# A ring of five half supergroups for x, one buffer for transposed channels, and all second weights in the ring

## The chip, the cores and the metric

The kernel runs on one core of one Trainium2 chip. Its five engines have their own instruction queues: PE (matrix multiply, with PEld for its weight loads), DVE (vector), ACT (scalar), POOL and SP, which here issues all transfers. The metric is the time of one execution on the device in microseconds (us).

## The reference

Two layers follow one another, in float32. The first is a causal convolution whose seven taps are different for every token and head; the second is a soft mixture of experts over all 28672 tokens.

```python
# x [8, 3584, 192], weight_gen [8, 3584, 8 heads, 7 taps]
w = softmax(weight_gen, axis=-1)
out[b, s, h, :] = sum_k w[b, s, h, k] * x_pad[b, s + k, h, :]      # 24 channels a head

x = out.reshape(28672, 192)
logits = x @ phi                                                    # 32 slots, 4 for each of 8 experts
slot_input = softmax(logits, axis=0).T @ x                          # over the tokens
slot_out[e] = relu(slot_input[e] @ w1[e]) @ w2[e]                   # 192 -> 1024 -> 192
return softmax(logits, axis=1) @ slot_out
```

## The kernel before

**Units of work.** A block is 26 tokens. A *group* is four blocks, 104 tokens, and a batch has 35 groups, so there are 280. Seven groups make a *supergroup* (40 of them, `s`), the piece in which x and the taps are loaded. Two neighbouring groups make a *pair* `p`, on which the engines work. Eight pairs make a *unit* `u` for the experts' softmax over tokens; the last two units have six.

**x.** The convolution is a matmul: `conv(p)` (L227 to 240) multiplies a band matrix of taps by 32 rows of x for each block. Heads are handled four at a time on 128 partitions, so x stands block-diagonally: head h of four on partitions 32h to 32h+31, in its own fourth of the columns, and zeros elsewhere. The zeros are written once (L138 to 141 and L394 to 397), and `loadx` (L170 to 174) overwrites the diagonal with four transfers of 32 rows. The tile `big` has room for two supergroups of x. A supergroup is loaded in two parts: part 0 is groups 0 to 3 (100 KB a transfer), part 1 groups 4 to 6 (75 KB). A part of supergroup s+2 goes where that part of s was, once PE has read it.

**Taps.** `loadw(s)` brings the taps of a supergroup into one of four buffers. From there a chain runs over several engines: `tap_top` (DVE, L184: maximum over seven taps), `tap_spread` (POOL, L190), `tap_rows` (PE, L196), `tap_sub` (DVE, L201), `tap_exp` (ACT, L205), `band_make` (POOL, L214), which writes one of three band buffers in halves.

**From a convolution to the experts.** `conv(p)` writes one of three PSUM buffers `cv`, p modulo 3. ACT takes the softmax denominators from it (L248), DVE inverts them (`conv_inv`, L254), and `conv_out(p)` (DVE, L259) divides and stores the pair as `tm`, after which `cv` is free for `conv(p + 3)`. PE transposes the pair (`xpose`, L273), ACT copies the result into `cm` (L278), the transposed channels of a unit, of which there are two buffers. When a unit is complete, `logits` (PE, L302) reads `cm`, the maximum is updated, and `dispatch` (L366) accumulates the slots' inputs.

**What sets the order.** The first pairs are written out by hand (from L377). The stream after that is a list of operations with a cost, what they read and what they write. A planner runs through it four times with these costs and then issues every operation at its planned time. PE's and SP's order is that of the list; DVE's, ACT's and POOL's is the planner's. On the chip each engine goes through its queue in order and waits on semaphores, so an instruction that waits holds up all that stand behind it. SP's transfers share eight landing semaphores in turn, so a transfer also waits for the landing of the one issued eight places before it. In the list, step k handles pairs 2k and 2k+1, and the loads for which x or taps buffers come free at that step stand in it:

```python
if part == 1 and s + 5 < NSG:
    op(SP, 0.4, [], [("w", (s + 5) % NTAP), ("r", (s + 5) % NTAP)], loadw, s + 5, late=4.2)
if s + 2 < NSG:
    op(SP, 1.8, [], [x_of(s, part)], loadx, s + 2, part, late=2.2)
```

**The end.** The second weights w2 of seven experts are loaded into `big` as x leaves it (`loadw2`, L454), those of the eighth into a tile of their own, `w2l` (L704 and 705). After the experts (L781), `big` serves a third time, as a ring of output buffers: PE makes output columns, DVE and ACT copy them into `big` (L809), SP sends them out.

## Time and profile before

| | |
|---|---|
| median of 3 runs | 349.42 us (348.41 to 350.35) |
| profiled execution: its own time, its span | 349.6 us, 347.9 us |
| mean granted clock of TensorE | 0.942 |
| PE, DVE, POOL, ACT busy | 311.6, 251.3, 215.3, 159.5 us |
| x loads: 160 of 100 KB, 160 of 75 KB | 3.5 and 4.1 us to landing (median) |
| taps loads: 40 of 392 KB | 4.4 us to landing (median) |

The span has a first fill (to some 30 us), the stream of pairs (to 260 us), the experts (to 286 us), and the output (to the end). In rows of groups, the columns are line, engine, operation, tiles and shapes, count, busy time and mean; an idle time in square brackets in a timeline row is that of the engine before the row, with what ended it. A row of a timeline may merge several instructions (x2). A matmul in float32 leaves two records, so `conv(p)`, sixteen matmuls, shows as x32, and a group as x16.

### The profile page before, as it was taken

How to read it: one execution, taken by the hardware profiler on the slowest of the kernel's cores; microseconds unless marked ns; L12 is line 12 of the kernel's file. 1: busy time of each engine (PE TensorE's matmuls, PEld its weight loads, DVE VectorE, ACT ScalarE, POOL GpSimd, SP SyncE). 2: the span in 40 equal slices, each digit the busy share in tenths (PEclk: the TensorE clock that was granted, in tenths of full speed). 3: DMA queues.
4: the chain of work that ended last, by engine and by line, in shares of the span. 5: the costliest groups of instructions: out<-in, count | busy, mean ns of one | idle time of the engine just before them, and what ended most of it. 6: DMA issues, size and time to landing. Idle time of an engine off the chain costs nothing.

```text
span 347.9 us, 16181 instructions
## 1 busy us (share of the span) xinstructions
PE 311.6 (90%) x6800; PEld 218.0 (63%) x6800; DVE 251.3 (72%) x550; ACT 159.5 (46%) x425; POOL 215.3 (62%) x259
## 2 busy tenths in 40 slices
PE   8799899989999999998999989899998789999810
PEld 6477777768777777786786867677776453233200
DVE  7677678787888888788887778777765639766520
ACT  6354355555556445645555435454550316344310
POOL 8699659879699878879797687796503610000000
PEclk9899999999999999999999999999999989886855
DMA  6887777858777867878768768665379009999995
GB/s 196 239 222 233 217 216 213 229 146 234 226 213 235 234 181 192 206 231 225 201 179 222 226 186 242 187 196 149 105 286 412 32 2 367 400 402 398 400 401 209
DMA packets 32856, 80.80 MB, mean 232 GB/s; under 512 B 7056, under 2 KB 7184, under 8 KB 32784
## 3 DMA queue, kind: packets, MB, share of 16 engines
q1 hardware_dynamic: 32784, 79.77, 72.9%
q8 instruction: 54, 0.88, 1.1%
q14 instruction: 18, 0.15, 0.1%
HBM read 57.38 MB, written 22.36 MB: 229 GB/s over the span
## 4 chain that ended last, share of the span: by engine, by line
PE 58%; DMA 13%; DVE 9%; POOL 6%; ACT 4%; issue 3%; SPq 3%; DVEq 0%; ACTq 0%; POOLq 0%
PE cv L238 22%; PE pt L273 11%; PE ls L302 6%; DMA out<-big 6%; PE pmx L196 6%; PE acb L366 5%; POOL band L214 4%; DMA taps<-wh 4%; PE po L802 4%; DMA big<-xh 4%; SPq L811 2%; PE so L781 2%; DVE tm L259 1%; DVE big L809 1%; SPq L174 1%
## 5 line engine op out<-in xcount | busy, mean ns | idle before, releaser
L214 POOL TENSOR_TENSOR band<-taps,mask 128x588 f32<-128x588 f32 (+3 forms) x158 | 139.2, 912 | 27.3 <-ACT taps L205 24.8
L238 PE MATMUL cv<-big,band 128*26 128x100 f32 x4480 | 117.4, 250 | 8.8 <-DMA big<-xh 4.7
L238 PEld LDWEIGHTS cv<-big,band 128*26 128x26 f32 x4480 | 95.7, 104 | 39.3 <-issue 30.5
L259 DVE TENSOR_TENSOR tm<-cv,ws 128x384 f32<-128x384 f32 x140 | 73.0, 551 | 6.5 <-DVE ws L254 0.5
L278 ACT COPY cm<-pt 128x312 f32<-128x312 f32 x140 | 52.1, 423 | 41.9 <-PE pt L273 41.1
L248 ACT ACTIVATE ws<-cv,eps 128x16 f32<-128x16 f32 x140 | 38.1, 273 | 64.0 <-PE cv L238 51.7
L273 PE MATMUL pt<-ident,tm 122*128 122x122 f32 x420 | 60.0, 279 | 0.7 <-ACT cm L278 0.7
L273 PEld LDWEIGHTS pt<-ident,tm 122*128 122x128 f32 x420 | 44.0, 142 | 17.7 <-issue 14.7
L802 PE MATMUL po<-cT,so 32*128 32x442 f32 (+3 forms) x256 | 44.4, 701 | 3.1 <-DVE big L809 2.0
L254 DVE RECIPROCAL ws<-ws 128x32 f32<-128x32 f32 x70 | 24.1, 344 | 27.1 <-ACT ws L248 26.5
L809 DVE COPY big<-po 128x936 f32<-128x936 f32 (+1 forms) x24 | 26.2, 1096 | 16.8 <-DMA out<-big 7.5
L809 ACT COPY big<-po 128x936 f32<-128x936 f32 (+1 forms) x24 | 21.8, 918 | 33.4 <-DMA out<-big 15.1
L190 POOL TENSOR_TENSOR spread<-own,top 128x392 f32<-128x392 f32 x37 | 31.3, 847 | 6.9 <-PE pt L273 2.8
L196 PE MATMUL pmx<-spread,near 128*128 128x392 f32 x80 | 34.3, 510 | 0.9 <-DVE maskT L391 0.7
L802 PEld LDWEIGHTS po<-cT,so 32*128 32x128 f32 (+1 forms) x256 | 14.2, 182 | 32.2 <-DVE big L809 14.8
L184 DVE TENSOR_REDUCE top<-taps 128x56 f32<-128x392 f32 x40 | 22.2, 556 | 11.2 <-DMA taps<-wh 9.2
L302 PE MATMUL ls<-cm,phi_sb 128*32 128x208 f32 (+1 forms) x576 | 28.6, 333 | 0.0
L366 PE MATMUL acb<-tm,dt 128*32 128x193 f32 x536 | 26.0, 328 | 1.0 <-issue 0.7
L205 ACT ACTIVATE taps<-taps 128x392 f32<-128x392 f32 x40 | 21.0, 525 | 9.9 <-DVE taps L201 9.8
L201 DVE TENSOR_TENSOR taps<-taps,pmx 128x392 f32<-128x392 f32 x40 | 22.1, 553 | 1.5 <-PE pmx L196 1.1
L79 POOL TENSOR_TENSOR LT<-LT,rm 128x576 f32<-128x576 f32 (+1 forms) x16 | 18.1, 1136 | 7.1 <-DVE rm L77 5.2
L91 POOL TENSOR_TENSOR LT<-LT,sm 128x576 f32<-128x576 f32 (+1 forms) x16 | 18.2, 1136 | 6.5 <-DVE sm L89 4.5
(113 smaller groups left out, 253.3 us busy)
## 6 DMA issues: line engine op xcount, KB each, us to landing
big<-xh SPq DMA_DIRECT2D x160, 100.0 KB, 3.5
taps<-wh SPq DMA_DIRECT2D x40, 392.0 KB, 4.4
big<-xh SPq DMA_DIRECT2D x160, 75.0 KB, 4.1
out<-big SPq DMA_DIRECT2D x24, 468.0 KB, 6.5
out<-big SPq DMA_DIRECT2D x24, 442.0 KB, 6.6
big<-w SPq DMA_DIRECT2D x7, 768.0 KB, 8.5
w1a_sb<-w1a SPq DMA_DIRECT2D x16, 256.0 KB, 4.6
w1b_sb<-w1b SPq DMA_DIRECT2D x8, 256.0 KB, 3.9
```

The costliest lines, as they stand in the source:

```text
L190: eng.tensor_tensor(out=tops[s][0], in0=own.to_broadcast([128, KT, NBC]), in1=tops[s][1].rearrange("p l o -> p o l").to_broadcast([128, KT ...
L196: P.matmul(pmx[:, 0:TAPS], near, tops[s][0].rearrange("p q l -> p (q l)"), start=True, stop=True)
L214: eng.tensor_tensor(out=w[:, :, z].rearrange("p b (a k) -> p b a k", k=k), in0=r[:, :, :, 0:k].to_broadcast([128, hi - lo, a, k]), in1=m[: ...
L238: P.matmul(cv[32 * blk : 32 * blk + T, o : o + 4 * GX], bands[s % NBAND][:, bc // 2, :, bc % 2], xb[:, :, bc * GX : (bc + 1) * GX], start= ...
L248: A.activation(wss[p // 2][:, p % 2], cvs[p % NCV][:, 0 : 16 * GX].rearrange("p (h w) -> p h w", w=GX)[:, :, GW:], AF.Identity, bias=eps[: ...
L259: V.tensor_tensor(out=tms[u % NTM][:, pr, 1 : 2 * D + 1].rearrange("p (h w) -> p h w", w=GW), in0=cv[:, :, 0:GW], in1=wss[p // 2][:, p % 2 ...
L273: P.transpose(pt[:, i, 0:TR], tm[0:TR, pr, 1 + 128 * i : 129 + 128 * i], ident[0:TR, 0:TR])
L278: copy(cms[u][:, pr].rearrange("p i b j -> p (i b) j"), pts.pop(p).rearrange("p i (b j) -> p (i b) j", j=32)[:, :, 0:T])
L302: P.matmul(lp[32 * blk : 32 * blk + 32, 0:n, par, 0:T], phi_sb[:, 2 * par + i, :], cm[:, 0:n, 1 if i else 2 * par, blk, :], start=(i == 0) ...
L366: P.matmul(ac[32 * q : 32 * q + 32], dt[:, g, :], tm[:, g // 2, o : o + D + 1], start=(g < 4), stop=(g + 4 >= 2 * n))
L802: P.matmul(po[dst : dst + hi - lo, q % 2, 0 : n * T], so[32 * q : 32 * q + 32, lo:hi], cT[32 * q : 32 * q + 32, g0 : g0 + n, 0:T], start=T ...
L809: (V.tensor_copy if done[1] % 2 else A.copy)(ot.rearrange("p (q c) -> p q c", q=2), po[:, :, 0 : n * T])
```

## The change

The tile `big` now holds five halves of a supergroup, numbered j = 2s + part, each 28 of the 56 block-columns (3.5 groups, 87.5 KB a transfer). `loadx(j)` fills slot j modulo 5. The first five halves are loaded before the stream, and half j + 5 goes where half j was. The fourth group of a supergroup now reads from two halves. The zeros of the fifth slot are four more operations, two on POOL and two on ACT. `big` grows by a quarter, from 44800 to 56000 bytes a partition. `cm` has one buffer instead of two, which frees 9984 bytes. All eight second weights go into `big` (12288 of its 14000 columns), and `w2l` is gone. The output ring has 14 buffers where it had 11.

```diff
-    XB = 4 * NBC * GX
-    big = keep.tile([128, 2 * XB], F32, name="big")
+    NXH, HBC = 5, NBC // 2
+    XB = 4 * HBC * GX
+    big = keep.tile([128, NXH * XB], F32, name="big")
...
-    xbd = [big[:, i * XB : (i + 1) * XB].rearrange("p (h c) -> p h c", h=4) for i in range(NXB)]
+    xbd = big.rearrange("p (i h c) -> p i h c", i=NXH, h=4)
...
-    def loadx(s, part):
-        xb = xbd[s % NXB]
-        z = slice(0, 8 * SGH * GX) if part == 0 else slice(8 * SGH * GX, NBC * GX)
+    def loadx(j):
+
+        s, part = divmod(j, 2)
+        z = slice(part * HBC * GX, (part + 1) * HBC * GX)
         for h in range(4):
-            SY.dma_start(xb[32 * h : 32 * h + 32, h, z], xh[s, h, :, z])
+            SY.dma_start(xbd[32 * h : 32 * h + 32, j % NXH, h], xh[s, h, :, z])
...
-                             xb[:, :, bc * GX : (bc + 1) * GX], start=True, stop=True)
+                             xbd[:, j % NXH, :, b * GX : (b + 1) * GX], start=True, stop=True)
...
-            cms[u] = pa.tile([128, UP, 3, 4, T], F32, tag="cm", name=f"cm{u}")
+            cms[u] = pa.tile([128, UP, 3, 4, T], F32, tag="cm", name=f"cm{u}", bufs=1)
...
+    for h in (0, 1):
+        G.memset(xbd[:, 4, h], 0.0)
...
+    for h in (2, 3):
+        A.copy(xbd[:, 4, h], zero.to_broadcast([128, HBC * GX]))
     band_make(0, 16, HB, V)
+    loadx(4)
     loadw(4)
...
         for s in range(NSG):
             for part in range(2):
-                if max(1, (SGG * s + (SGH, SGG)[part] - 1) // 4) != k:
+                j = 2 * s + part
+                if max(1, (SGG * s + (3, 6)[part]) // 4) != k:
                     continue
...
-                if s + 2 < NSG:
-                    op(SP, 1.8, [], [x_of(s, part)], loadx, s + 2, part, late=2.2)
-                elif s == NSG - 2 and part == 1:
-                    op(SP, 2.0, [], [x_of(s, 0), x_of(s, 1)], loadw2, 0, XB // WE, late=8.0)
+                if j + NXH < 2 * NSG:
+                    op(SP, 1.8, [], [x_of(j)], loadx, j + NXH, late=2.2)
+                elif j + 2 < 2 * NSG:
+                    i = j + NXH - 2 * NSG
+                    op(SP, 1.0, [], [x_of(j)], loadw2, i * XB // WE, (i + 1) * XB // WE)
...
-    op(SP, 2.0, [], [x_of(0, 0), x_of(0, 1), x_of(1, 0), x_of(1, 1)], loadw2, XB // WE, E - 1)
+    op(SP, 2.0, [], [x_of(j) for j in range(NXH)], loadw2, 3 * XB // WE, E)
...
-    w2l = pc.tile([128, WE], F32, name="w2l", bufs=1)
-    SY.dma_start(w2l, w2[:, E - 1])
...
-    OT = 2 * XB // (2 * 18 * T)
+    OT = NXH * XB // (2 * 18 * T)
```

What this does to the queues is seen on SP first. Before, from the taps of supergroup 2 on (a row with x4 is one part of x, and the number in taps0 to taps3 is the buffer; the second load of taps0 is that of supergroup 4):

```order
L177 DMA taps2_86<-wh 128x784
L177 DMA taps3_87<-wh 128x784
L174 DMA big_67<-xh 32x800 x4
L174 DMA big_67<-xh 32x600 x4
L409 DMA phi_sb_62<-phi 128x128
L177 DMA taps0_84<-wh 128x784
L174 DMA big_67<-xh 32x800 x4
L177 DMA taps1_85<-wh 128x784
L174 DMA big_67<-xh 32x600 x4
L174 DMA big_67<-xh 32x800 x4
L177 DMA taps2_86<-wh 128x784
```

And with the change, the same stretch:

```order
L177 DMA taps2_86<-wh 128x784
L177 DMA taps3_87<-wh 128x784
L174 DMA big_67<-xh 32x700 x8
L411 DMA phi_sb_62<-phi 128x128
L174 DMA big_67<-xh 32x700 x4
L177 DMA taps0_84<-wh 128x784
L174 DMA big_67<-xh 32x700 x4
L177 DMA taps1_85<-wh 128x784
L174 DMA big_67<-xh 32x700 x8
L177 DMA taps2_86<-wh 128x784
```

Each taps load from that of supergroup 4 on has four more x transfers ahead of it, counted from the start. In the stream the same pattern goes on: one half of x, the taps, the other half.

On POOL, the two memsets of the fifth slot stand between those of the third and fourth and the bands of supergroup 1. Before:

```order
L394 MEMSET big_67 128x1400
L396 MEMSET big_67 128x1400
L397 MEMSET big_67 128x1400
L214 TENSOR_TENSOR band1_89<-taps1_85,mask2_130 128x6x42
L214 TENSOR_TENSOR band1_89<-taps1_85,mask2_130 128x6x10
```

And with the change:

```order
L394 MEMSET big_67 128x2x700
L396 MEMSET big_67 128x2x700
L397 MEMSET big_67 128x2x700
L399 MEMSET big_67 128x700 x2
L214 TENSOR_TENSOR band1_89<-taps1_85,mask2_130 128x6x42
L214 TENSOR_TENSOR band1_89<-taps1_85,mask2_130 128x6x10
```

ACT's two copies stand after the denominators of the second pair, ahead of its copies into `sel4`. Apart from these rows, the forms of the zeroing and the eighth weights' source, the orders of PE, DVE, ACT and POOL are as before.

More of the change, by code (lines that the diff above doesn't have):

```diff
@@ L101, in conv_soft_moe @@
     ps_l = actx.enter_context(tc.tile_pool(name="ps_l", bufs=1, space=PSUM))
[L103 to L104 removed]
+    NTM, NCV, NTAP, NBAND = 2, 3, 4, 3
+    xbd = big.rearrange("p (i h c) -> p i h c", i=NXH, h=4)
     HB = NBC // 2
@@ L137, in conv_soft_moe @@
     V.memset(one, 1.0)
-    V.memset(xbd[0][:, 0, :], 0.0)
-    G.memset(xbd[0][:, 1, :], 0.0)
-    V.memset(xbd[0][:, 2, :], 0.0)
-    A.copy(xbd[0][:, 3, :], zero.to_broadcast([128, NBC * GX]))
+    V.memset(xbd[:, 0:2, 0], 0.0)
+    G.memset(xbd[:, 0:2, 1], 0.0)
+    V.memset(xbd[:, 0:2, 2], 0.0)
+    A.copy(xbd[:, 0:2, 3], zero.unsqueeze(1).to_broadcast([128, 2, HBC * GX]))
     ident = keep.tile([128, 128], F32, name="ident")
@@ L378, in conv_soft_moe @@
     loadw(1)
-    loadx(0, 0)
-    loadx(0, 1)
+    loadx(0)
+    loadx(1)
     loadw(2)
@@ L393, in conv_soft_moe @@
     tap_top(1)
-    G.memset(xbd[1][:, 3, :], 0.0)
-    A.copy(xbd[1][:, 1, :], zero.to_broadcast([128, NBC * GX]))
-    G.memset(xbd[1][:, 0, :], 0.0)
-    G.memset(xbd[1][:, 2, :], 0.0)
+    G.memset(xbd[:, 2:4, 3], 0.0)
+    A.copy(xbd[:, 2:4, 1], zero.unsqueeze(1).to_broadcast([128, 2, HBC * GX]))
+    G.memset(xbd[:, 2:4, 0], 0.0)
+    G.memset(xbd[:, 2:4, 2], 0.0)
+    for h in (0, 1):
+        G.memset(xbd[:, 4, h], 0.0)
     tap_sub(0)
@@ L406, in conv_soft_moe @@
     loadw(3)
-    loadx(1, 0)
-    loadx(1, 1)
+    loadx(2)
+    loadx(3)
     SY.dma_start(phi_sb, phi)
@@ L487, in op, with x_of @@
         ops.append((eng, cost, late + 0.1 * (eng == "TE"), preds, due, f, a))
-    def x_of(s, part):
-        return ("x", s % NXB, part)
+    def x_of(j):
+        return ("x", j % NXH)
     def band_of(s, half):
@@ L498, in conv_reads @@
             s, g = divmod(g, SGG)
-            r |= {x_of(s, int(g >= SGH))} | {band_of(s, h) for h in range(2)
+            r |= {x_of(2 * s + h) for h in range(2) if (g < 4, g > 2)[h]} | {band_of(s, h) for h in range(2)
                                               if (g < 4, g > 2)[h]}
@@ L510, in conv_soft_moe @@
         op(AC, 0.6 - 0.3 * (q % 2), [], ["sel4"], sums, q)
-    for late, what in ((1.0, ("x", 1, 0)), (1.7, ("x", 1, 1)), (0.0, ("w", 2)), (1.0, ("w", 3)),
-                       (4.0, ("w", 4 % NTAP)), (0.0, ("band", 1, 0)), (2.5, ("band", 1, 1))):
+    for late, what in ((1.0, x_of(2)), (1.7, x_of(3)), (0.0, ("w", 2)), (1.0, ("w", 3)),
+                       (4.0, ("w", 4 % NTAP)), (5.0, x_of(4)), (0.0, ("band", 1, 0)), (2.5, ("band", 1, 1))):
         op(SP, 0.0, [], [what], lambda: None, late=late)
@@ L559, in conv_soft_moe @@
             n = UNITS[v][1]
-            op(TE, 0.2 * n - 0.07, [("cm", v % 2, pr) for pr in range(n)], ["ls"], logits, v)
+            op(TE, 0.2 * n - 0.07, [("cm", pr) for pr in range(n)], ["ls"], logits, v)
             op(VE, 0.85, [], ["ls", "mq", "acb"], top, v)
@@ L571, in conv_soft_moe @@
                 op(TE, 0.34, [tm_of(i)], [("pt", i % 2)], xpose, i)
-                op(AC, 0.4, [], [("pt", i % 2), ("cm", *tm_of(i)[1:])], xpose_out, i)
+                op(AC, 0.4, [], [("pt", i % 2), ("cm", unit(i)[1])], xpose_out, i)
                 continue
@@ L603, in conv_soft_moe @@
         op(TE, 0.34, [tm_of(p)], [("pt", p % 2)], xpose, p)
-        op(AC, 0.4, [], [("pt", p % 2), ("cm", *tm_of(p)[1:])], xpose_out, p)
+        op(AC, 0.4, [], [("pt", p % 2), ("cm", unit(p)[1])], xpose_out, p)
     op(VE, 0.6, [], ["dd", "dt"], dturn, v)
@@ L609, in conv_soft_moe @@
     op(TE, 0.37, ["dt", *tmv], ["acb"], dispatch, v, 0, 4)
-    op(TE, 1.1, [("cm", final % 2, pr) for pr in range(UNITS[final][1])], ["ls"], logits, final)
+    op(TE, 1.1, [("cm", pr) for pr in range(UNITS[final][1])], ["ls"], logits, final)
     op(VE, 0.7, [], ["ls", "mq"], top, final)
@@ L703, in conv_soft_moe @@
     pb = ctx.enter_context(tc.tile_pool(name="pb", bufs=1))
-    w2l = pc.tile([128, WE], F32, name="w2l", bufs=1)
-    SY.dma_start(w2l, w2[:, E - 1])
     def w2_at(e, f):
-        return (w2l if e == E - 1 else big[:, e * WE : (e + 1) * WE])[:, f * D : (f + 1) * D]
+        return big[:, e * WE + f * D : e * WE + (f + 1) * D]
     ps_b = bctx.enter_context(tc.tile_pool(name="ps_b", bufs=1, space=PSUM))
```

4 lines of the change are left out of this document (1 added, 3 removed).

## The prediction

> **What bounds the kernel now.** I began with the windows of busy time, to see which engine the long middle stage hangs on, and then read the chain and the table of waits for what the change aims at.
>
> ```profile
> 90.00:120.00 30.00, 29.27 (x752) 22.59 (x750) 24.73 (x60) 16.64 (x51) 25.64 (x30) 1.00 0.80 233
> PE cv L238 22%; PE pt L273 11%; PE ls L302 6%; DMA out<-big 6%; PE pmx L196 6%; PE acb L366 5%; POOL band L214 4%; DMA taps<-wh 4%; PE po L802 4%; DMA big<-xh 4%; SPq L811 2%; PE so L781 2%; DVE tm L259 1%; DVE big L809 1%; SPq L174 1%
> PE cv L238 <- DMA big<-xh: 4.7, 5, 1.4
> DVE top L184 <- DMA taps<-wh: 9.2, 11, 2.6
> SPq L174 <- PE cv L238: 26.2, 29, 2.8
> ```
>
> The columns of the first row are the window, then the busy time of PE, PEld, DVE, ACT and POOL, the clock, the DMA share and GB/s. PE is busy for 29.27 of 30 us at full clock, so in the stream only idle PE time is to be had. The chain gives 4% of the span to x loads (big<-xh), and the table of waits says that PE's convolutions waited 4.7 us in five places for x. That is the time a deeper ring could take away, if the label is right. A wait for several semaphores is put down to whichever moved last, so I looked at the places themselves.
>
> The longest in the stream is at 71.28 us. It is conv(35), the first of supergroup 10 (sixteen weight loads a group, counted from the start). It needs x of that supergroup's first part, the bands, and its accumulator buffer, which conv(32) used before it and which conv_out(32) must have emptied.
>
> ```profile
> 61.83 2.10 SPq L174 DMA_DIRECT2D big<-xh  x4
> DMA to landing us min/median/max: 2.8/3.0/3.3
> 69.58 0.56 DVE L184 TENSOR_REDUCE top<-taps 128x56 f32<-128x392 f32 x1 [1.31 <-DMA taps<-wh]
> 70.51 1.02 DVE L259 TENSOR_TENSOR tm<-cv,ws 128x384 f32<-128x384 f32 x2
> 71.28 0.55 PE L238 MATMUL cv<-big,band 128*26 128x100 f32 x16 [1.19 <-DMA big<-xh]
> ```
>
> The first two rows are the four loads of that x and their time to landing: issued by 63.93, landed by 67.2 at the latest, 4 us before use. The label is wrong. DVE stood 1.31 us at the tap maximum, waiting for a taps load, with conv_out(32) behind it. That is the first of the two in the row at 70.51 and ends at 71.02 to 71.07; PE goes on 0.2 us later. Two more stalls have the same form:
>
> ```profile
> 118.71 0.56 DVE L184 TENSOR_REDUCE top<-taps 128x56 f32<-128x392 f32 x1 [1.02 <-DMA taps<-wh]
> 119.56 0.56 DVE L259 TENSOR_TENSOR tm<-cv,ws 128x384 f32<-128x384 f32 x1
> 120.33 0.59 PE L238 MATMUL cv<-big,band 128*26 128x100 f32 x17 [0.72 <-DMA big<-xh]
> 219.81 0.56 DVE L184 TENSOR_REDUCE top<-taps 128x56 f32<-128x392 f32 x1 [1.21 <-DMA taps<-wh]
> 220.66 0.56 DVE L259 TENSOR_TENSOR tm<-cv,ws 128x384 f32<-128x384 f32 x1
> 221.43 0.38 PE L238 MATMUL cv<-big,band 128*26 128x100 f32 x8 [1.00 <-DMA big<-xh]
> ```
>
> Each time DVE stands at a late taps load, conv_out ends (120.12, 221.22), and PE resumes 0.21 us after it. So 1.19 + 0.72 + 1.00 = 2.9 of the 4.7 us belong to taps, by way of DVE's order. Is x ever late? From all of it:
>
> ```profile
> L238 PE MATMUL cv<-big,band x4096: 246/248/277, 30.8 to 257.4; 128*26 128x100 f32 x196
> DMA to landing us min/median/max: 1.9/3.8/5.6
> 14.09 0.74 PE L238 MATMUL cv<-big,band 128*26 128x100 f32 x16 [1.37 <-DMA big<-xh]
> 40.27 0.55 PE L238 MATMUL cv<-big,band 128*26 128x100 f32 x16 [0.46 <-DMA big<-xh]
> ```
>
> The 4096 records are 256 groups in 226.6 us: 0.885 us a group. A part of x is freed 10 or 11 groups before its successor is needed, which is 8.9 us at least. Four issues (2.1 us in the row above) and the longest landing of all x loads (5.6) take 7.7 us. So 1.2 us are left in the worst case, as long as SP comes to the load in time. What remains under x's name is 1.37 us at 14.09, in the first fill, where nothing had to be freed, and 0.46 us at 40.27.
>
> **The change part by part.** *Five halves instead of two supergroups.* The successor of a half is now needed 13 or 14 groups later, so 8.9 us become 11.5. By the rows above this is slack on slack: the term is 0. Bounds: 0, and the whole label after the fill, 4.7 - 1.37 = 3.3 us gained. I take 0, since three of the four stalls have another owner.
>
> What decides is whether taps come earlier. In the order of SP's transfers the taps load of supergroup s+5 stands, before and now, behind the four loads that wait for the same event: PE through the fourth group of s. Its second condition, the bands of s+1, is untouched. In the stream each taps load is issued as before: 0. The transfers keep their number, and 100 and 75 KB become 87.5 KB.
>
> *The first fill.* Here the order differs: the fifth half goes ahead of the fifth taps load (T4), which was ahead of x.
>
> ```profile
> 13.82 0.36 SPq L177 DMA_DIRECT2D taps<-wh  x1
> 14.29 1.76 SPq L174 DMA_DIRECT2D big<-xh  x4
> DMA to landing us min/median/max: 3.5/3.5/3.5
> DMA to landing us min/median/max: 3.2/4.4/5.8
> 18.41 0.55 DVE L184 TENSOR_REDUCE top<-taps 128x56 f32<-128x392 f32 x1
> 20.12 1.02 DVE L259 TENSOR_TENSOR tm<-cv,ws 128x384 f32<-128x384 f32 x2
> 20.57 1.58 PE L238 MATMUL cv<-big,band 128*26 128x100 f32 x64
> 23.14 0.93 PE L196 MATMUL pmx<-spread,near 128*128 128x392 f32 x2 [0.21 <-POOL spread L190]
> ```
>
> The landings are T4's alone, then those of all taps. T4 now issues 1.76 + 0.11 us later, at 15.7. It lands at 18.9 with the shortest landing, 19.2 with its own, 20.1 with the median, 21.5 with the longest. DVE wants it at 18.41, and behind it stand conv_out(4) and (5), the pair at 20.12. I take 3.9 us, between its own and the median, since four x loads now lie ahead of it: 19.6, and DVE is 1.3 us late. The second convolution of the pair at 20.57 begins near 21.36. Its buffer comes free at 20.63 + 0.2, so 0.53 us are covered; PE's wait for POOL at 23.14 swallows another 0.21. Left: 1.3 - 0.74 = **+0.5 us**, bounds 0 and 21.5 + 0.1 - 18.41 - 0.74 = +2.4. The next taps load also follows four x loads. It issues near 17.9 and lands at 22.3 with the median, before DVE, now late, reaches its maximum. The one after waits for POOL's bands, as before.
>
> The stall at 14.09 waits for the third x part, now 350 KB instead of 400. Twelve per cent of the 1.76 us of four such loads is 0.2; I take **-0.1**, bounds -0.3 and 0.
>
> *Zeroing the fifth half.*
>
> ```profile
> 7.13 1.26 POOL L397 MEMSET big<- 128x1400 f32 x1
> 9.61 4.53 POOL L214 TENSOR_TENSOR band<-taps,mask 128x252 f32<-128x252 f32 x6 [1.22 <-ACT taps L205]
> 14.32 0.30 ACT L443 COPY selE<-ident 32x128 f32<-32x128 f32 x1 [3.18 <-POOL selE L426]
> ```
>
> POOL gets two memsets of 700 columns, half of 1.26 us each, in a 1.22 us gap: 0.04 us over, taken as 0. Without the gap it would be 1.26. ACT's two copies fall into its 3.18 us gap. SP's four new loads follow both by time: 0.
>
> *One buffer for the transposed channels.*
>
> ```profile
> 28.35 1.77 PE L302 MATMUL ls<-cm,phi_sb 128*32 128x208 f32 x32
> 30.05 0.84 PE L273 MATMUL pt<-ident,tm 122*128 122x122 f32 x6
> 30.62 0.74 ACT L278 COPY cm<-pt 128x312 f32<-128x312 f32 x2 [1.52 <-PE pt L273]
> ```
>
> The copies into the buffer must now wait for the logits that read it. They wait already: their transposes stand behind those logits on PE, and the orders of PE, ACT and DVE do not move in the stream. Cost 0. Were it not so, it would be up to 1.77 us for each of 17 later units.
>
> *Second weights in the ring, and more output buffers.*
>
> ```profile
> L456 SPq DMA_DIRECT2D big<-w x7: 328/433/1196, 253.1 to 259.4; - x7
> DMA to landing us min/median/max: 4.6/8.5/10.6
> w2l<-w SPq DMA_DIRECT2D x1, 768.0 KB, 5.4
> 282.26 0.62 PEld L781 LDWEIGHTS so<-w2l,hT 128*32 128x32 f32 x16
> 288.00:340.00 52.00, 41.52 (x234) 12.93 (x232) 31.71 (x34) 20.09 (x22) 0.00 (x0) 0.76 1.02 400
> ```
>
> The eighth matrix joins the seven. Even behind them (259.4 + 10.6 + 5.4 = 275.4) it lands before its use at 282.26. The output runs at 400 GB/s with the DMA engines full, so 14 buffers instead of 11 end at the same time. Both 0.
>
> **Sum**, against the profiled execution's 349.6 us (span 347.9 and 1.7 around it): 349.6 + 0.5 - 0.1 = 350.0. The median of the runs is 0.2 below that execution, so I forecast **349.8 us**.
>
> **The rivals.** *The label is right (0.14).* PE does wait for x, by partial landings that my reading of the last one misses. Then 3.3 us go: 349.4 - 3.3 + 0.4 = 346.5. For it speak five waits under one name, recurring some 50 us apart; against it the landing at 67.2. A rule of the Trainium skill takes its side (Perfetto Trace Analysis, "Optimization Strategy"): the same gap repeating on an engine that should be saturated can mean too little SBUF for the next tile. By that rule the time would be the one just given; the trace has the repeating gap, but the buffers that the three gaps wait for are accumulators, not x.
>
> *The taps loads fall differently (0.08).* The stalls come from taps that are about 1 us late. Transfers shifted by four places may put slow issues elsewhere, and two of the three stalls vanish: 349.8 - 2 = 347.8. Nothing aims at it.
>
> *The fill costs more (0.14), the other side.* T4 takes the longest landing, DVE stands 3.1 us with conv_out behind it, and PE loses 2.4: 349.4 + 2.4 = 351.8. It decides once T4 lands after 19.2 (18.41 + 0.74), and is over the half per cent if it lands after 20.9. Taps loads of 5.4 us and more are in the rows, so it is possible; T4's own 3.5 speaks against.
>
> *The single buffer serialises (0.02):* 349.4 + 17 x 1.77 = 379. PE's order rules it out.
>
> **How the numbers follow.** The forecast has 0.62, with its own range 348.4 to 350.9 by the spread of the runs. About half a per cent (1.7 us) is what a measurement here can tell from none. The range 347.2 to 351.6 takes in the forecast, the shifted taps and most of the costly fill; it leaves out 0.13 of the right label and part of the rest. Faster by over 0.5%: 0.13 from the label and 0.05 from shifted taps and spread, 0.18. Slower: 0.09 from the fill, 0.02 from the buffer, 0.02 from spread, 0.13. The rest, 0.69, is no change.
>
> **What would show it.** Right, if the profile after still has PE waits of 0.7 to 1.2 us in the stream, each behind a DVE maximum that waits for taps, and DVE's wait for taps stays near 9 us, while x lands 4 us or more ahead of use. The step on the fill shows in the row of the fifth tap maximum (18.41 before): a wait for taps of about 1.3 us, and PE behind by half a microsecond at 23. I am wrong if the stream's PE waits vanish with taps as late as now, or if DVE's wait for taps changes by several microseconds.

## The result and the profile after

The changed kernel takes 353.56 us (median of six, 350.72 to 358.02) where the kernel before takes 349.88 us on the same chip (six, 348.41 to 356.14). The ratio is 1.011 with a 95% interval of 1.0064 to 1.0156: it is slower, by about 1%. I had forecast 349.8 us and a range up to 351.6.

The six executions of either kernel spread over some 2%, and a ratio takes only those within 1.5% of the fastest (there is none where a single one is left), so I give the medians of all executions beside each ratio. As a measure of what a comparison can tell: the kernel before, run against itself, came out at 0.9954 (0.9914 to 0.9993). So half a per cent is nothing.

The profiled execution took 355.31 us, with a span of 353.6. Its chain of waits, in shares of the span:

```profile
PE cv L238 20%; PE pt L273 10%; DMA taps<-wh 9%; PE ls L302 6%; DMA out<-big 5%; PE pmx L196 5%; PE acb L366 4%; POOL band L214 3%; DMA big<-xh 3%; DVE big L814 3%; PE po L807 3%; SPq L174 3%; PE so L786 2%; DVE cT L456 1%; DVE tm L259 1%
```

And its table of waits (total, times, longest):

```profile
DVE top L184 <- DMA taps<-wh: 15.4, 13, 3.1
PE cv L238 <- POOL spread L190: 4.0, 2, 2.1
PE cv L238 <- DMA big<-xh: 3.6, 3, 1.4
PE cv L238 <- DVE tm L259: 2.9, 4, 1.1
```

The taps loads' share of the chain has grown from 4% to 9%, and DVE's wait for them from 9.2 to 15.4 us. PE's waits are spread over three names now, but look at the longest, 2.1 us under POOL's name. From DVE's and PE's timelines of the changed kernel around it:

```profile
174.24 0.56 DVE L184 TENSOR_REDUCE top<-taps 128x56 f32<-128x392 f32 x1 [2.61 <-POOL band L214]
175.16 1.02 DVE L259 TENSOR_TENSOR tm<-cv,ws 128x384 f32<-128x384 f32 x2
175.93 0.89 PE L238 MATMUL cv<-big,band 128*26 128x100 f32 x32 [2.11 <-POOL spread L190]
```

It is the pattern that the prediction found under x's name: DVE stands at a tap maximum, for a load that was issued at 169.29 and landed 4.86 us later, at 174.15 (POOL, named in the row, ended its bands at 174.20; but the maximum starts 0.09 us after the landing, as those at T5 and T7 below do, so the 2.61 us belong to taps, though the 15.4 don't hold them). Two conv_outs stand behind it, and PE goes on 0.3 us after the first of them has ended (175.16 and half of 1.02). At these places the labels mislead in either kernel; the DVE row ahead of the gap tells more.

Where were the microseconds lost? The rows of the experts' logits are a good clock, since PE's order is the same in both kernels. The third of them in the kernel before, and the last start of all (the end of "first and last start"):

```profile
57.14 1.62 PE L302 MATMUL ls<-cm,phi_sb 128*32 128x208 f32 x32
...
L302 PE MATMUL ls<-cm,phi_sb x576: 293/338/364, 28.3 to 261.6; 128*32 128x208 f32 x171, 128*32 128x156 f32 x21
```

The same in the changed kernel:

```profile
59.60 1.61 PE L302 MATMUL ls<-cm,phi_sb 128*32 128x208 f32 x32
...
L302 PE MATMUL ls<-cm,phi_sb x576: 293/338/553, 29.5 to 267.4; 128*32 128x208 f32 x171, 128*32 128x156 f32 x21
```

So 2.5 us are lost by 57 us, 5.8 by the last logits, and the rest of the span is alike (86.3 and 86.2 us). The first part lies in the fill. SP's timeline of the kernel before has the three taps loads after T4 at

```profile
16.16 0.36 SPq L177 DMA_DIRECT2D taps<-wh  x1
...
22.30 0.35 SPq L177 DMA_DIRECT2D taps<-wh  x1
...
27.39 0.74 SPq L177 DMA_DIRECT2D taps<-wh  x1
```

and that of the changed kernel, from the fifth half on, reads

```profile
14.23 1.77 SPq L174 DMA_DIRECT2D big<-xh  x4
16.09 0.37 SPq L177 DMA_DIRECT2D taps<-wh  x1
16.55 1.77 SPq L174 DMA_DIRECT2D big<-xh  x4
18.42 0.37 SPq L177 DMA_DIRECT2D taps<-wh  x1
18.89 5.59 SPq L174 DMA_DIRECT2D big<-xh  x8
24.61 0.35 SPq L177 DMA_DIRECT2D taps<-wh  x1
...
30.47 0.36 SPq L177 DMA_DIRECT2D taps<-wh  x1
```

T4 is issued 2.27 us later than before, T5 2.26, T6 2.31, T7 3.08. Nothing takes up the shift by four transfers: T10, issued at 45.92 before and at 48.30 now, is still 2.38 us later. DVE and PE, in their timelines of the changed kernel, show what that does:

```profile
19.65 0.56 DVE L184 TENSOR_REDUCE top<-taps 128x56 f32<-128x392 f32 x1 [0.76 <-DMA taps<-wh]
24.24 0.56 DVE L184 TENSOR_REDUCE top<-taps 128x56 f32<-128x392 f32 x1 [1.37 <-DMA taps<-wh]
35.73 0.56 DVE L184 TENSOR_REDUCE top<-taps 128x56 f32<-128x392 f32 x1 [2.07 <-DMA taps<-wh]
...
23.65 0.83 PE L196 MATMUL pmx<-spread,near 128*128 128x392 f32 x2
25.87 0.89 PE L238 MATMUL cv<-big,band 128*26 128x100 f32 x32 [0.57 <-DVE tm L259]
37.28 0.92 PE L238 MATMUL cv<-big,band 128*26 128x100 f32 x30 [1.08 <-DVE tm L259]
```

The row at 23.65 was at 23.14 before. That looks like the half microsecond that I forecast for T4, but most of it isn't T4's, as told below. What follows, at T5 and T7, I had costed at nothing.

### The profile page after: what moved, and what is told of

It is laid out like the page before. It is cut to its first block, busy times and chain, and to the rows that moved or that the text cites. A ratio compares the mean times of both kernels' runs of the same rounds, so it can differ in the third digit from the quotient of the medians.

```text
span 353.6 us, 16152 instructions
## 1 busy us (share of the span) xinstructions
PE 311.8 (88%) x6800; PEld 220.0 (62%) x6800; DVE 250.5 (71%) x550; ACT 161.0 (46%) x427; POOL 216.6 (61%) x261
## 4 chain that ended last, share of the span: by engine, by line
PE 52%; DMA 17%; DVE 11%; POOL 5%; issue 4%; ACT 3%; SPq 3%; DVEq 0%; POOLq 0%; ACTq 0%
PE cv L238 20%; PE pt L273 10%; DMA taps<-wh 9%; PE ls L302 6%; DMA out<-big 5%; PE pmx L196 5%; PE acb L366 4%; POOL band L214 3%; DMA big<-xh 3%; DVE big L814 3%; PE po L807 3%; SPq L174 3%; PE so L786 2%; DVE cT L456 1%; DVE tm L259 1%
## 5 line engine op out<-in xcount | busy, mean ns | idle before, releaser
L238 PE MATMUL cv<-big,band 128*26 128x100 f32 x4480 | 118.4, 249 | 13.2 <-POOL spread L190 4.0
L807 PE MATMUL po<-cT,so 32*128 32x468 f32 (+3 forms) x256 | 42.3, 737 | 1.4 <-DVE big L814 0.7
L184 DVE TENSOR_REDUCE top<-taps 128x56 f32<-128x392 f32 x40 | 22.2, 556 | 18.4 <-DMA taps<-wh 15.4
L807 PEld LDWEIGHTS po<-cT,so 32*128 32x128 f32 (+1 forms) x256 | 14.7, 191 | 28.0 <-ACT big L814 12.5
L302 PE MATMUL ls<-cm,phi_sb 128*32 128x208 f32 (+1 forms) x576 | 30.8, 345 | 0.1
L302 PEld LDWEIGHTS ls<-cm,phi_sb 128*32 128x32 f32 x576 | 20.7, 111 | 4.5 <-issue 0.7
## 6 DMA issues: line engine op xcount, KB each, us to landing
big<-xh SPq DMA_DIRECT2D x320, 87.5 KB, 3.7
```

The source lines that it names most:

```text
L238: P.matmul(cv[32 * blk : 32 * blk + T, o : o + 4 * GX], bands[s % NBAND][:, bc // 2, :, bc % 2], xbd[:, j % NXH, :, b * GX : (b + 1) * GX] ...
L302: P.matmul(lp[32 * blk : 32 * blk + 32, 0:n, par, 0:T], phi_sb[:, 2 * par + i, :], cm[:, 0:n, 1 if i else 2 * par, blk, :], start=(i == 0) ...
L807: P.matmul(po[dst : dst + hi - lo, q % 2, 0 : n * T], so[32 * q : 32 * q + 32, lo:hi], cT[32 * q : 32 * q + 32, g0 : g0 + n, 0:T], start=T ...
```

## The experiments

**How the kernels compare.** For each kernel: the medians of all executions (with that of the kernel before in the same comparison), the ratio with its interval, and from one profile DVE's wait for taps before and after 48 us and the matmul records between 60 and 240 us, a rough count of how far the stream gets in 180 us.

| kernel | median, before (us) | ratio | DVE's wait, us | records |
|---|---|---|---|---|
| before | | | 1.3, 7.9 | 4490 |
| before, again | 347.76, 349.94 | 0.9954 (0.9914 to 0.9993) | 0, 8.6 | 4508 |
| changed | 353.56, 349.88 | 1.011 (1.0064 to 1.0156) | 4.7, 10.7 | 4390 |
| changed, second | 354.79, 348.99 | 1.022 (1.0125 to 1.0315) | 6.1, 13.9 | 4392 |
| changed, third | 356.17, 349.94 | 1.017 (1.0111 to 1.0229) | 6.3, 10.3 | 4340 |
| changed, ring of four halves | 351.05, 349.25 | 0.9983 (0.9928 to 1.0038) | 2.5, 10.8 | 4519 |
| before, four scrap transfers | 350.51, 349.25 | 0.9998 (0.9958 to 1.0038) | 6.0, 11.5 | 4460 |
| changed, T4 first | 352.25, 348.99 | 1.0184 (1.009 to 1.0278) | 4.3, 11.4 | 4480 |
| changed, fill of before | 352.27, 349.23 | 1.0075 (1.0041 to 1.0109) | 1.4, 12.5 | 4458 |
| before, taps first | 347.92, 348.99 | 1.0034 (0.9984 to 1.0083) | 1.3, 0.8 | 4572 |
| changed, taps first | 348.98, 348.99 | none | 1.8, 0 | 4680 |
| the same again | 347.95, 349.94 | 0.9948 (0.9914 to 0.9981) | 0.6, 2.3 | 4543 |
| changed, fifth half late | 345.75, 349.94 | 0.9903 (0.9866 to 0.9941) | 5.8, 1.0 | 4599 |
| the same, w1 later | 344.56, 349.23 | 0.9885 (0.9847 to 0.9924) | 2.6, 6.7 | 4616 |
| changed, taps by ACT | 350.33, 350.34 | 0.9991 (0.9953 to 1.0028) | 4.0, 5.0 | 4497 |
| fifth half late, taps by ACT | 355.25, 350.34 | 1.0165 (1.0105 to 1.0224) | 6.3, 6.9 | 4492 |

**1. Only the fifth half undone.** The changed kernel, its halves, single `cm`, w2 and output buffers kept; with the fifth half its zeroing goes as well (parts of the edit left out are marked ...):

```diff
-    NXH, HBC = 5, NBC // 2
+    NXH, HBC, NR = 5, NBC // 2, 4
...
-            SY.dma_start(xbd[32 * h : 32 * h + 32, j % NXH, h], xh[s, h, :, z])
+            SY.dma_start(xbd[32 * h : 32 * h + 32, j % NR, h], xh[s, h, :, z])
...
-    for h in (0, 1):
-        G.memset(xbd[:, 4, h], 0.0)
...
-    for h in (2, 3):
-        A.copy(xbd[:, 4, h], zero.to_broadcast([128, HBC * GX]))
     band_make(0, 16, HB, V)
-    loadx(4)
     loadw(4)
...
-                if j + NXH < 2 * NSG:
-                    op(SP, 1.8, [], [x_of(j)], loadx, j + NXH, late=2.2)
+                if j + NR < 2 * NSG:
+                    op(SP, 1.8, [], [x_of(j)], loadx, j + NR, late=2.2)
```

> The changed kernel with the ring cut to four halves; single buffer, halves, w2 in the ring and 14 output buffers stay. Theory A (the loss comes from the fifth half: its four transfers stand ahead of the fifth taps load and SP's queue stays behind until 45 us): as fast as the kernel before, about 349.9 us (349.2 to 350.6), T4 issued near 13.9 us, DVE's wait for taps near 9 us. Rival B (the loss comes from the other edits: single buffer, equal halves, w2): it stays near 353.5 us.

It runs as the kernel before does, by the ratio; by the medians it is 1.8 us above, which is the edge of what these comparisons tell. So of the 3.7 to 6.2 us that the changed kernel loses by its medians, none by the ratio and at most 1.8 us by the medians belong to equal halves, one `cm` buffer, w2 and the output ring together. The rest is the fifth half, its zeroing included. DVE's wait for taps, 13.2 us in all, isn't near the 9 us that theory A named.

The zeroing can be read from the profile of the changed kernel:

```profile
10.01 4.53 POOL L214 TENSOR_TENSOR band<-taps,mask 128x252 f32<-128x252 f32 x6 [0.37 <-ACT taps L205]
14.72 0.30 ACT L448 COPY selE<-ident 32x128 f32<-32x128 f32 x1 [1.80 <-POOL selE L431]
```

Behind the two memsets POOL still stands for 0.37 us, and behind its two copies ACT for 1.80 us, so both fit into the gaps. The fastest kernels below have this zeroing too.

**2. Four more transfers, nothing else.** In the kernel before:

```diff
+    scrap = keep.tile([128, NBC // 2 * GX], F32, name="scrap")
...
+    for h in range(4):
+        SY.dma_start(scrap[32 * h : 32 * h + 32], xh[2, h, :, 0 : NBC // 2 * GX])
     loadw(4)
```

> The kernel before, and four more transfers of 87.5 KB into a scrap tile that nobody reads, ahead of the fifth taps load. Nothing else changes. Theory A: the fifth taps load lands near 19.6 us instead of 17.3, PE is 2 to 3 us behind at 45 us and the time is 2 to 3 us above the kernel before, near 352.4 us. If half of the loss belongs to the stream and only the fill's part comes back here, this number is that part. Rival B: four transfers are absorbed as forecast, +0.5 us or less, near 350.2 us.

The table of DVE's waits before 48 us:

```profile
DVE top L185 <- DMA taps<-wh: 6.0, 5, 1.8
```

Four transfers that nobody reads raise DVE's wait in the fill from 1.3 to 6.0 us, just what the changed kernel has (4.7 to 6.3). That is the cause of the waits in the fill. But the time did not follow as theory A wanted: the third logits stand at 57.93, where the kernel before has 57.14 and 56.30, and the ratio is 1.000. So these waits alone don't make the loss. What covered them on PE here I did not follow.

**3. The taps ahead of x, first try.** Both kernels, with each taps load moved ahead of the part of x that it stood behind:

```diff
-        ops[i][5](*ops[i][6])
+        f, a = ops[i][5:]
+        if f is loadx and a[0] % 2 and (a[0] + 5) // 2 < NSG:
+            loadw((a[0] + 5) // 2)
+        if f is not loadw or a[0] == 4:
+            f(*a)
```

(This is the changed kernel's; in the kernel before, the conditions are `a[1] == 0` and `a[0] + 3`.)

> The changed kernel; each taps load from the sixth on stands ahead of the half of x that it stood behind by one half (about 3 us earlier in SP's queue). Orders of PE, DVE, ACT and POOL unchanged. Theory A (gaps of the stream come from late taps by way of DVE's order, x has 4 us and more to spare): DVE's wait for taps falls from 15.4 us to 2 to 5 us, what remains lies in the fill, time 346 to 349 us. Rival C (the gaps named after x or after POOL's spread are what they say): DVE's wait falls but the time stays within 1 us of the changed kernel's 353.6.

> The kernel before with the same move of the taps loads ahead of x. Theory A: DVE's wait for taps falls from 9.2 us to 1 to 3 us, the time by 2 to 4 us to 346 to 348 us; x, whose least slack was 1.1 us, pays 0.4 us of issue and the taps' share of the transfers and stays in time. Rival D (the ring of two supergroups is too short for it): x becomes late, PE waits for x with no DVE wait ahead of it, time 349 us or more; then the deeper ring is what makes the move possible.

In these two, the loads of supergroups 6 and 7 stand ahead of the bands of 2 and 3, which are made from the same buffers: these bands get the wrong taps, and POOL waits for loads that it should not need. POOL's waits in the changed kernel so edited:

```profile
POOL band L214 <- DMA taps<-wh: 5.2, 1, 5.2
```

The times (351.24 and 352.79 us against 349.25; ratios 1.0047, 1.0008 to 1.0087, and 1.0095, 1.0057 to 1.0133) hold that loss, and say nothing on the question. They do show the price of moving a transfer past the last reader of its buffer.

**4. T4's place, and taps first where the buffer is free.** The changed kernel with T4 back ahead of the fifth half; then in addition the taps loads of supergroup 5 and of 8 and later one half of x earlier, where the bands made from their buffers stand ahead of them in the program; and the same second edit in the kernel before. The first edit is

```diff
+    loadw(4)
     loadx(4)
-    loadw(4)
```

and the second

```diff
+    banded, early = {0, 1}, set()
...
+        if f is band_make and a[2] == HB:
+            banded.add(a[0])
+        n = (a[0] + 5) // 2 if f is loadx and a[0] % 2 else 0
+        if n and n < NSG and n not in early and n - 4 in banded:
+            loadw(n)
+            early.add(n)
+        if f is not loadw or a[0] not in early:
+            f(*a)
```

> The changed kernel itself once more, beside the other three and the kernel before on one chip. Theory A1 (the change costs what the first comparison says, by more than four scrap transfers cost): ratio to before 1.006 to 1.015, PE 2 to 3 us behind at 45 us again, DVE's wait for taps near 15 us. Theory A2 (most of the 1.1% was scatter of where slow taps loads fall, since the ring cut to four came out at 0.998 and the four extra transfers at 1.000): ratio 0.998 to 1.005, and PE within 1.2 us of the kernel before at 45 us.

> The changed kernel with one edit: the fifth taps load ahead of the fifth half of x, as in the kernel before. Theory A (order in the first fill): T4 lands near 17.4 us and DVE's fifth tap maximum is not late; PE is 1 to 1.5 us less behind at 45 us than in the changed kernel, since the sixth and later taps loads still have four more transfers ahead; ratio to before 1.002 to 1.008. If the stream alone is to blame (rival S): same time as the changed kernel. If the fill is all of it and T4 is all of the fill: 0.998 to 1.002.

> The changed kernel with the fifth taps load ahead of the fifth half, and each later taps load one half of x earlier in SP's queue as soon as the bands that it overwrites are written out ahead of it. Orders of PE, DVE, ACT and POOL unchanged. Theory A: DVE's wait for taps falls to 2 to 5 us and with it PE's gaps in the stream; 345 to 348 us, ratio 0.987 to 0.997. Rival C (PE's gaps are not made by late taps): ratio above 1.003.

> The kernel before with the same move of taps loads ahead of x. Theory A: DVE's wait for taps falls from 9 us to 1 to 4 us, x stays in time with less slack; 346 to 348 us, ratio 0.990 to 0.998. Rival D (the ring of two supergroups is too short once taps go first): PE waits for x that follow no late DVE work, 2 us or more in sum, ratio 1.000 or above; then the deeper ring is what lets taps go first.

The changed kernel repeats its result: 5.8 us above the kernel before, third logits at 59.63 and last at 267.3 (59.60 and 267.4 the first time). So the loss is no accident of one profile. With T4 first, the median is 2.5 us lower and the third logits come at 58.64, but the ratios, 1.018 and 1.022, can't be told apart, and 1.018 lies above the 1.002 to 1.008 of theory A. DVE's waits in the fill are still 4.3 us, now at the loads behind T4.

Taps first does to DVE's wait and to PE's gaps what theory A says. The busy times of the changed kernel with it, 60 to 240 us (window, PE, PEld, DVE, ACT, POOL, clock, DMA share, GB/s):

```profile
60.00:240.00 180.00, 179.46 (x4680) 139.23 (x4678) 151.85 (x357) 97.53 (x292) 154.95 (x174) 1.00 0.75 214
```

Those of the changed kernel as it is:

```profile
60.00:240.00 180.00, 172.36 (x4390) 132.72 (x4383) 142.19 (x335) 91.28 (x273) 148.00 (x166) 0.99 0.74 205
```

PE idles for 0.5 us instead of 7.6, and 290 more matmul records fall into the window. The transfers are as many as before, and no engine's order but SP's was touched; DVE's wait for taps after 48 us is gone. The profiled execution took 341.75 us, but the five others 348.0 to 352.0, so the gain of that profile can't be taken for the kernel's: its median of 348.98 us is 5.8 us below the changed kernel's on the same chip, level with the kernel before, and above the 345 to 348 of theory A.

In the kernel before, the same move takes DVE's wait from 9.2 to 2.1 us in all, and now x is on the edge. PE's waits after 48 us there:

```profile
PE cv L238 <- DMA big<-xh: 3.2, 3, 1.7
```

The least time from a landing of x to its use fell from 1.1 to 0.1 us in the stream (from the landing and first weight load of each part). So rival D is half right, and the ratio (1.0034) is the one that it named: with two supergroups the taps can go first only at x's expense, and the ring of five is what would pay for it. In the changed kernel as it is the least is 3.7 us, and nothing spends it.

**5. The fifth half late.** The ring of five, but SP's order that of the kernel before: the fifth half isn't loaded in the fill, and each half goes into a slot that came free one half earlier.

```diff
-    loadx(4)
     loadw(4)
...
-        ops[i][5](*ops[i][6])
+        f, a = ops[i][5:]
+        if f is loadx:
+            f(a[0] - 1)
+        elif f is loadw2 and a[0] == 0:
+            loadx(2 * NSG - 1)
+            f(*a)
+        else:
+            f(*a)
```

> The kernel before once more, for a second profile of it. Theory A3 (in the stream each taps load races with DVE's tap maximum by a margin of about nothing, so the stalls of one profile are partly luck): DVE's wait for taps lies between 9 and 15 us and PE's progress to the end of the stream within 2 us of the first profile's. Theory S (the ring of five itself makes taps later in the stream): it is 9 to 10 us again, with the 9.2 of the first profile.

> The changed kernel without the fifth half in the first fill: SP's order is that of the kernel before again, each half goes to the slot that came free one half earlier, so SP no longer stands before x for PE, and the taps load behind it issues up to 3 us earlier. Orders of PE, DVE, ACT and POOL unchanged. Theory A: DVE's wait for taps falls from 15 to 20 us to 2 to 6 us, PE is within 1 us of the kernel before at 45 us, 345 to 348 us or a ratio to before of 0.985 to 0.997. Rival E (the window of eight transfers in flight, not PE, holds SP): taps come no earlier, ratio 0.998 to 1.005.

> The changed kernel with the taps loads ahead of x once more, on one chip with the changed kernel and with the late fifth half. Theory A: DVE's wait for taps near 2 us again, PE busy for 29.5 of each 30 us or more between 60 and 240 us, 4 to 8 us below the changed kernel, ratio to before 0.98 to 1.0. If the first profile of it was luck: DVE's wait 8 us or more, as slow as the kernel before.

> The changed kernel, third time, for the comparison on this chip. Theory A: DVE's wait for taps 15 to 20 us, PE 2 to 3 us behind the kernel before at 45 us, 5 to 7 us behind at the end of the stream, ratio 1.008 to 1.02. Theory A3 lets the stream's part of it vary by 2 to 3 us.

The kernel before repeats its wait for taps (8.6 us, a little under the 9 to 15 of theory A3) and reaches its last logits 1.9 us earlier, within the 2 us of A3; the changed kernel repeats its loss.

The fifth half late is the clearest comparison: 345.75 us (343.93 to 347.25), 10 us below the changed kernel's 356.17 on the same chip, and below the kernel before by 1% (by 0.6% against the median of its repetition, 347.76). The ring, its size and every engine's order but SP's are those of the change. What differs is what the spare half is spent on. In the change it is spent on x, which lands one half earlier and needs it nowhere. Here it is spent on SP: a load of x more often finds its slot free, so SP stands less, and the taps load behind it goes out earlier. SP's wait for PE before loads of x, from the table of waits:

```profile
SPq L174 <- PE cv L238: 17.3, 25, 2.0
```

That was 26.2 us in the first profile of the kernel before, and 19.0 in the second. The label splits one wait over several lines of PE; over all of them it is 28.8 us here, 31.2 to 38.2 in the changed kernel's three profiles, and 41.7 and 41.0 in the kernel before. On average over supergroups 10 to 39, a taps load is issued 7.3 us before DVE wants it, where the kernel before and the changed kernel have 4.9 to 5.0, and takes about as long to land (4.4 us, against 4.3 to 4.6). Taps land 2.9 us before DVE has reached their maximum (its landing against the start of the maximum less the idle time before it), where the kernel before has 0.4 and 0.6 us in its two profiles and the changed kernel 0.6, 0.4 and 0.7. These spread by 1.3 to 1.7 us from load to load. So at 0.5 us every load is a race, and DVE waits 11 to 16 times in forty; at 2.9 us it waits once after 48 us, for 1.0 us. The fill of this profile went badly all the same: DVE stood 4.0 us at one load (T9) and PE 2.9 us behind it, and the third logits came at 60.36.

Taps first, the second time, gave 347.95 us, within half a per cent of the kernel before by its ratio, though DVE waited for 2.9 us only. In that profile PE was late from the start: first logits at 31.1, where the profile before this had 28.7.

**6. The fill alone undone, and the fill relieved.** In the first run, the fifth half is held back and SP's order is that of the kernel before up to the sixteenth half; then two halves come together, and from there the order is the changed kernel's. In the second, the fifth half is late as above, and the loads of w1 begin three supergroups later (`4 + 3 * j // 2 == s` for `1 + 3 * j // 2 == s`).

```diff
-    loadx(4)
     loadw(4)
...
+        if f is loadx and a[0] <= 16:
+            f(a[0] - 1)
+        if f is not loadx or a[0] >= 16:
+            f(*a)
```

> The changed kernel with the fill of the kernel before: the fifth half is not loaded at the start, each half up to the sixteenth comes one place later in SP's queue, then two come together and from there, near 55 us, the order is that of the changed kernel. Theory F (the fill makes the loss): DVE's wait for taps before 48 us at 2 us or less, the time 347 to 350.5 us, ratio to before 0.995 to 1.003, though the stream's waits for taps stay at 8 to 12 us. Theory S (the order of the ring of five costs in the stream by itself): DVE's wait after 48 us at 10 us or more, PE loses 2 to 4 us against the kernel before between 60 and 240 us, ratio 1.006 to 1.012.

> The version with the late fifth half, and the loads of the first weights begin three supergroups later, so four or five transfers less stand in SP's queue between 20 and 48 us. Theory Q (SP's queue is full in the fill, and what is taken out of it brings taps earlier): DVE's wait for taps before 48 us falls from 5.8 us to 0 to 3 us, time 343 to 346 us, ratio to before 0.980 to 0.990. Rival: the waits there come from slow landings, not from SP's queue: they stay at 4 us or more and the time near 345.8.

The first lies between my two theories: DVE's wait in the fill is gone (1.4 us) and 352.27 us is about half way back, yet 0.75% stays. It doesn't divide the loss cleanly either, for its third logits are late again (59.14), ahead of the pair of halves, which comes at 46.85. The weight loads' row and a row of POOL's timeline say what PE stood for:

```profile
40.77 0.35 PEld L238 LDWEIGHTS cv<-big,band 128*26 128x26 f32 x16 [2.03 <-POOL band L214]
36.58 3.52 POOL L214 TENSOR_TENSOR band<-taps,mask 128x588 f32<-128x588 f32 x4 [0.32 <-ACT taps L205]
```

PE waited for POOL's bands. Taps have a part in it, by the other way in which they reach PE: a maximum that waited 0.51 us at 32.95, its rows and its exponent after it, then the bands. But POOL stood for that exponent for 0.32 us only, so most of the 2.03 us has another cause, which I did not follow.

The second is the fastest kernel of all: 344.56 us, ratio 0.9885, all six executions (342.78 to 346.05) below all of the kernel before (346.25 and up). Its waits for taps in the fill fell from 5.8 to 2.6 us, as SP's crowded queue would have it. In the stream they rose from 1.0 to 6.7, so it isn't simply the late fifth half made better.

**7. The taps out of SP's queue.** ACT issues each taps load from the sixth on, in the changed kernel and in the one with the fifth half late.

```diff
-        SY.dma_start(taps[s % NTAP], wh[s])
+        (SY if s < 5 else A).dma_start(taps[s % NTAP], wh[s])
```

> The changed kernel, each taps load from the sixth on issued by ACT, at the place that the planner gave it, instead of SP. x, the fill's order on SP and all else unchanged. Theory A (the loss is taps behind x in SP's queue): DVE's wait for taps after 48 us falls from 10 to 14 us to 3 us or less, in the fill from 5 or 6 us to 3 or less, time 344 to 348 us, ratio 0.985 to 0.997; ACT loses 35 issues of some 0.4 us, which its idle time covers. Rival X (the ring's x costs by itself, or ACT then stands before the transfers' window and holds up what is behind it): ratio 1.003 or above, with PE waiting for ACT.

> The version with the late fifth half, taps issued by ACT in the same way. Theory A: the fill's remaining wait of 5.8 us before 48 us shrinks to 3 us or less, since SP's queue no longer holds the taps up; 343 to 346 us, ratio 0.980 to 0.990. Rival X: as above, slower than the 345.75 us of the late fifth half with taps on SP.

With x of the ring of five untouched and only the taps off SP's queue, the kernel is as fast as the kernel before (350.33 against 350.34 us). That fits a loss made on SP's queue. But the forecast of theory A, 344 to 348 us with waits of 3 us or less, was missed (4.0 and 5.0 us), and the same move in the kernel before was not run: whether ACT's issues would speed that up too, and so hide a cost of the ring, is open. The second run went against theory A, to 355.25 us, and the waits of ACT before 48 us show one reason, an engine that has computing to do standing behind an issue:

```profile
ACT ws L248 <- DMA taps<-wh: 3.9, 1, 3.9
```

What else it loses I did not follow.

## Why the prediction was wrong, point by point

**What bounds the kernel: right.** PE's gaps under x's name in the stream are gaps of DVE's order at late taps. A ring that gives x 3.7 us and more did not remove them; three ways of bringing taps earlier (taps first, the fifth half late, taps by ACT) cut DVE's wait after 48 us from 10 to 14 us down to 0 to 5, with x as deep (and in the kernel before, from 8 or 9 us to 0.8, with x shallower). The rival "the label is right" is out. The rule of the Trainium skill that I had set beside it (Perfetto Trace Analysis, "Optimization Strategy") says that the same gap repeating can mean too little SBUF or PSUM; I had named SBUF alone. As a reading of the label that led astray here: more SBUF for x alone lost 1%. The gaps did wait for an accumulator, which is in PSUM, but no run here has more of these. The paragraph before it in that section, to find what blocks the engine and make that start sooner, is what the fifth half late did.

**The first fill: the step that failed.** "The next taps load also follows four x loads. It issues near 17.9 and lands at 22.3 with the median, before DVE, now late, reaches its maximum. The one after waits for POOL's bands, as before." T5 was issued at 18.42 and took 5.73 us, not the median 4.4; it landed at 24.15 and DVE stood 1.37 us. The profile before had shown T5's own landing and the start of its maximum:

```profile
DMA to landing us min/median/max: 5.4/5.4/5.4
21.64 0.56 DVE L184 TENSOR_REDUCE top<-taps 128x56 f32<-128x392 f32 x1
```

Issued at 16.16, it had landed at 21.54, with 0.1 us to spare; a shift of 2.3 us could not be covered. The one after (T6) had waited for POOL before, but for 0.2 us only, until 22.30. Now it came at 24.61, 2 us after the bands were done (22.58), so the shift by four transfers went through the point that I had thought would stop it, and on to T7, where DVE stood 2.07 us. All three profiles of the changed kernel have such waits at T4, T5 and T7 (0.37 to 0.93, 1.07 to 1.37 and 0.88 to 2.07 us). In the two of the kernel before, and in the three with its order on SP in the fill (ring of four, fifth half late, fill of before), DVE doesn't wait at T4 and T5, and 0.5 us at most at T7; with w1 later, the fourth of this kind, it waits 0.1, 0.6 and 0.9 us.

My term for T4 itself was met by luck. It landed at 19.63, as forecast, but was issued 0.4 us later than I had worked out and landed 0.36 us faster; DVE, itself 0.4 us later since before T4 (the fourth maximum at 17.41, before 17.00), stood 0.76 us and not 1.3. And the row at 23.65 is no measure of T4: the same row is at 23.84 and 23.45 in the other two profiles of the changed kernel, at 23.30 in the second of the kernel before, and at 23.46 with the fifth half late, where T4 is in time. Against that last one, T4 alone cost PE 0 to 0.4 us.

The mistake was to cost one late load and not the queue. SP does pause: between 14 and 48 us it stood for 7.7 us in the kernel before and 7.2 in the changed one. But it paused for landings eight places earlier, for PE and for POOL, and these were late too: in the row at 18.89, SP waits for two landings, the second T5's own at 24.15. Instead of +0.5 the three profiles have the third logits at 59.60, 59.63 and 60.24, where the kernel before has 57.14 and 56.30: about +3. How much of that is the queue's shift stays open, since a profile with the order of before in the fill can be as late (60.36 with the fifth half late).

**"In the stream each taps load is issued as before: 0": the second step that failed.** The sentence is true of the margin, which is the same within its scatter (0.4 to 0.7 us in five profiles). But the stream of the changed kernel is slower in all three: from the third to the last logits 207.8, 207.7 and 209.4 us, against 204.5 and 203.4, so +3 to +6 in these profiled executions, the larger part of the loss, where I had put 0. And the promised sign, a wait near 9 us for taps, failed with 15.4, 20.0 and 16.6. Part of the loss is PE's clock. From the changed kernel, the windows around and behind the 2.11 us stall at 175.93:

```profile
173.80:176.70 2.90, 0.79 (x40) 0.80 (x40) 2.36 (x5) 0.43 (x2) 2.16 (x3) 1.00 0.80 210
176.70:180.20 3.50, 3.50 (x43) 2.34 (x33) 2.12 (x5) 0.47 (x2) 0.83 (x2) 0.51 0.73 225
180.20:183.00 2.80, 2.80 (x80) 2.08 (x79) 1.62 (x6) 1.81 (x5) 1.61 (x2) 1.00 0.04 13
```

For 3.4 us behind the stall the granted clock (third from the end) is halved, and 3.5 us hold 43 matmul records where the next 2.8 hold 80: some 1.7 us are lost again. The third profile has two such phases in this stretch, behind stalls of 2.01 and 2.40 us; the kernel before has none in it, in either profile, and no stall above 1.4 us. Not every long stall is followed by one (1.94 us at 74.51 in the changed kernel is not), and the second profile has none and is as slow. So this explains 1.7, 0 and 3.4 us. It also came in the fill, behind stalls of 1.78 us in that third profile, 2.91 us with the fifth half late and 1.83 us with the fill of before, and so made their third logits later.

Why a margin that is as good on average still loses the rest I have not settled. With the taps issued by ACT the same stretch takes 204.8 us, which points to SP's queue again; but with T4 first, where the order in the stream is that of the changed kernel to the last transfer, it takes 204.7 us. So the order in the stream isn't the whole of it, and what the fill leaves behind for the stream stays open.

**The other edits: right within what can be told.** One `cm` buffer, w2 and the output buffers are all in the ring of four, at a ratio of 0.998 and 1.8 us by medians; the zeroing fits into its gaps, as the rows there show. The stall at 14.09 for the third part of x, 1.37 us, is 1.17 now, within its bounds, though not for the reason given: four of the smaller loads take as long to issue (1.77 us against 1.76).

**The rivals.** "The fill costs more" had the right sign and place, and the wrong mechanism: it waited for T4 to land late (after 20.9 for half a per cent), but T4 landed at 19.63, and the loss came from those behind it. I gave slower 0.13, and the range ended 2 us below the result, because the bound of the fill's term was made from one load and the stream had no term at all.

## What to carry to other kernels

In a queue that is issued in order, ask what a deeper buffer lets the queue do next: the spare slot was worth up to 1% when it let SP move on to the load that was late, and cost 1 to 2% when it was filled at once, ahead of that load. Cost an added transfer at every load behind it, and at the margin that each of these has in the trace; a pause of the queue takes the shift up only if what it waits for isn't late by the same shift. When an engine's gap has a label with several possible releasers, look at the in-order engine beside it and at what stands at the head of its queue.

## What was not expected of the hardware

The time that SP takes to issue a transfer is mostly 0.4 us, but it isn't constant. The taps loads of the changed kernel, from the view of that tile (issue time in ns, least, median, longest):

```profile
L177 SPq DMA_DIRECT2D taps<-wh x40: 346/357/1334, 0.8 to 235.4; - x40
```

Of the 441 transfers some 40 take more than 0.7 us in each profile of the kernel before and of the changed one, mostly at other places each time: 43 of those issued before 262 us in the changed kernel, 37 us in sum beyond 0.42 each (counted over all its transfers), of which some 10 are waits for a semaphore; the rest follows no event that the trace shows. The row at 18.89 above holds one of them: eight transfers take 5.59 us where twice 1.77 is usual, 0.8 us of it in one slow issue and 1.4 us in waits for landings. With taps loads that have 0.5 us to spare on average, slow issues may decide which of them is late, and may be part of why single executions differ; no run here separates that.
